# The first product of a second MLP in seven block products for eight, fused with the second product

## The chip, the cores and the metric

The kernel runs on one core of a Trainium2 chip. The metric is device time in microseconds (us), the median of three runs. One further execution was profiled; all rows below come from it.

## The reference

A block retention (a linear attention with decay) feeds two MLPs, all in float32. Cut to what matters here:

```python
x = retention(q, k, v, lam)            # (1536 tokens, 512)
h = x @ moe_w_in                       # (1536, 2048)
x = (np.maximum(h, 0) + alpha * np.minimum(h, 0)) @ moe_w_out
h = x @ moe2_w_in                      # second MLP, first product
r = np.maximum(h, 0.0)
out = (r * r) @ moe2_w_out             # second MLP, second product: (1536, 512)
```

## The kernel before

Each MLP product of float32 operands is made from three matmuls in a faster float32 form: every operand is split into a high part and a low remainder, and low x high, high x low and high x high are added in PSUM.

The retention comes first. Then both MLPs run through one list of steps, 48 for each: a step is one token tile t (512 of 1536 tokens) and one block f of 128 hidden columns. `first` (L176) makes h of a step: 4 chunks of 128 input channels x 3 matmuls = 12 matmuls of 512 columns. `activate` applies the leaky or the squared relu (ScalarE, then VectorE), casts the high part gh on ScalarE (L195), and `rest` subtracts the low part gl on VectorE (L200). `second` (L229, L231) adds the step's share to four running sums in PSUM, 12 matmuls more, two steps later (`LAG`). The order of the steps (`PARTS`) visits a tile in parts; a part's sums that aren't final go through DRAM (`sums`) and are added on VectorE when the next part ends (`end_sum`, L245).

The weights arrive as 64-bit floats and are converted on the chip, one unit (512 values per partition) a step: two activations on ScalarE (L127, L128), three integer operations on VectorE (L134, L135, L143), a cast on ScalarE (L145), a subtraction on VectorE (L154). The sum of the first MLP for a tile stays in PSUM and is split from there into the next x (`next_x`).

The order of instructions on every engine is the order of the code; each engine works its own list in order, and semaphores join them. PSUM has 8 banks: three for h, five for the running sums.

Of the kernel before, what the change touches and what calls it, by code (L numbers as in the profile page):

```python
# [16 lines left out]
CH = 128  # L17
# [6 lines left out]
TT = 512  # L24
# [14 lines left out]
LAG = 2  # L39
ORDER = [(n // B, n % B) for n in range(NN)]  # L40
# [15 lines left out]


@with_exitstack
def retention_then_two_mlps(
# [19 lines left out]
    xp = ctx.enter_context(tc.tile_pool(name="xp", bufs=1))  # L79
    wpa = ctx.enter_context(tc.tile_pool(name="wpa", bufs=1))  # L80
    rawp = ctx.enter_context(tc.tile_pool(name="rawp", bufs=AHEAD))
    bitp = ctx.enter_context(tc.tile_pool(name="bitp", bufs=3))
    gp = ctx.enter_context(tc.tile_pool(name="gp", bufs=LAG + 1))
    tp = ctx.enter_context(tc.tile_pool(name="tp", bufs=1))
    pp = ctx.enter_context(tc.tile_pool(name="pp", bufs=4))
    dram = ctx.enter_context(tc.tile_pool(name="dram", bufs=1, space=bass.MemoryType.DRAM))

    alpha_sb = const.tile([128, NF], F32, name="alpha_sb")

# [110 lines left out]
    def second(m, t, f, part):  # L203
# [4 lines left out]
        if last and f == NF - 2:  # L208
            return
# [424 lines left out]
```

## Time and profile before

| | us |
|---|---|
| timed runs, median (lowest to highest) | 581.49 (581.03 to 581.57) |
| the profiled execution | 582.9 |
| its span, first to last instruction | 580.6 |
| TensorE busy | 572.1 (99%) |
| VectorE busy | 334.7 (58%) |
| ScalarE busy | 293.6 (51%) |

The span is what the profiler saw of instructions; the execution's own time has 2.3 us more around it. A busy share is a mean over stages. Matmuls are pipelined, so the duration listed for one is not the time from one to the next.

### The profile page before, as it was taken

To read this page: it belongs to the slowest core of one execution; us is meant where nothing else is said; L and a number is where in the kernel's file an instruction comes from. 1 tells how busy PE (TensorE), PEld (TensorE's weight loads), DVE (VectorE), ACT (ScalarE), POOL (GpSimd) and SP (SyncE) were. 2 spreads that over 40 slices of the span, in tenths; PEclk is the share of its full clock that TensorE was granted. 3 is DMA by queue.
4 is the path that set the end of the run, shared out by engine and by line. 5 is a ranking of instruction groups with operands and counts; after the bars stand their busy time and mean duration, and the time that the engine had idled before them with its cause. 6 is when DMAs were issued, how large, how long until landed. Compare 5 with 4: busy or idle time off the path is not lost.

```text
span 580.6 us, 7855 instructions
## 1 busy us (share of the span) xinstructions
PE 572.1 (99%) x3058; PEld 475.7 (82%) x3058; DVE 334.7 (58%) x535; ACT 293.6 (51%) x509; POOL 33.3 (6%) x34
## 2 busy tenths in 40 slices
PE   8998999999999999999999999999999999999997
PEld 7887888888888888888888888888888888888885
DVE  3888766666666666866866965665632222222422
ACT  2566765765746765765765654654522222322220
POOL 2785000000000000000000000000000000000000
PEclk9999999999999999999999999999999999999999
DMA  7993343323544223333333123423100000400401
GB/s 255 361 393 120 108 146 109 117 102 109 192 147 168 82 100 109 110 108 110 108 110 109 51 94 110 141 78 109 73 0 1 0 1 0 146 0 1 145 2 72
DMA packets 25732, 62.38 MB, mean 107 GB/s; under 512 B 2904, under 2 KB 3936, under 8 KB 25696
## 3 DMA queue, kind: packets, MB, share of 16 engines
q1 hardware_dynamic: 17488, 32.01, 15.7%
q10 hardware_dynamic: 8208, 29.89, 15.5%
q8 instruction: 24, 0.39, 0.3%
q14 instruction: 12, 0.10, 0.0%
HBM read 52.44 MB, written 9.45 MB: 107 GB/s over the span
## 4 chain that ended last, share of the span: by engine, by line
PE 95%; DMA 3%; DVE 1%; issue 0%; SPq 0%; DVEq 0%
PE h L176 45%; PE acc L231 22%; PE acc L229 22%; PE o L436 2%; PE o L444 2%; PE s L399 1%; DMA q<-in_qt_dram 1%; DMA r<-in_kr_dram 1%; DMA zd<-z 1%; PE pk L459 1%; DMA lam_sb<-in_lam_dram 0%; DVE err L358 0%; DVE ps L245 0%; SPq L304 0%; DVE low L359 0%
## 5 line engine op out<-in xcount | busy, mean ns | idle before, releaser
L195 ACT CAST gh<-g 128x512 fp32r<-128x512 f32 x96 | 59.6, 621 | 90.5 <-DVE g L186 37.5
L186 DVE SCALAR_TENSOR_TENSOR g<-h,g 128x512 f32<-128x512 f32 x48 | 33.2, 691 | 123.4 <-ACT g L185 123.4
L185 ACT ACTIVATE g<-h 128x512 f32<-128x512 f32 x48 | 28.7, 598 | 124.3 <-PE h L176 124.3
L200 DVE TENSOR_TENSOR gl<-g,gh 128x512 fp32r<-128x512 f32 x96 | 66.5, 692 | 30.3 <-ACT gh L195 21.6
L176 PE MATMUL h<-xah,wl 128*128 128x512 f32 x192 | 74.8, 390 | 0.0
L176 PE MATMUL h<-xah,wh 128*128 128x512 f32 x192 | 74.7, 389 | 0.0
L176 PE MATMUL h<-xal,wh 128*128 128x512 f32 x192 | 74.7, 389 | 0.0
L229 PE MATMUL acc<-gh,wl 128*128 128x512 f32 x192 | 74.7, 389 | 0.0
L229 PE MATMUL acc<-gh,wh 128*128 128x512 f32 x192 | 74.7, 389 | 0.0
L229 PE MATMUL acc<-gl,wh 128*128 128x512 f32 x192 | 74.7, 389 | 0.0
L176 PE MATMUL h<-xbh,wl 128*128 128x512 f32 x192 | 74.7, 389 | 0.0
L176 PE MATMUL h<-xbl,wh 128*128 128x512 f32 x192 | 74.7, 389 | 0.0
L176 PE MATMUL h<-xbh,wh 128*128 128x512 f32 x192 | 74.7, 389 | 0.0
L231 PE MATMUL acc<-wl,gh 128*128 128x512 f32 x192 | 74.7, 389 | 0.0
L231 PE MATMUL acc<-wh,gh 128*128 128x512 f32 x192 | 74.7, 389 | 0.0
L231 PE MATMUL acc<-wh,gl 128*128 128x512 f32 x192 | 74.7, 389 | 0.0
L190 DVE SCALAR_TENSOR_TENSOR g<-h,g 128x512 f32<-128x512 f32 x42 | 29.0, 691 | 62.2 <-ACT g L189 62.2
L135 DVE SCALAR_TENSOR_TENSOR bits<-raw,bits 128x512 uint32<-128x512 uint32 x64 | 46.9, 733 | 2.2
L154 DVE TENSOR_TENSOR wl<-bits,wh 128x512 fp32r<-128x512 f32 x64 | 44.6, 697 | 2.7 <-ACT wh L145 2.7
L143 DVE CUSTOM_DVE_ANT_0 bits<-raw,bits 128x1024 uint16<-128x1024 uint16 x64 | 46.0, 718 | 0.0
L127 ACT ACTIVATE bits<-raw 128x512 f32<-128x512 f32 x64 | 43.0, 672 | 0.7 <-DMA raw<-in_w_dram 0.6
L128 ACT ACTIVATE raw<-raw 128x512 int32<-128x512 uint32 x64 | 42.7, 667 | 0.0
(73 smaller groups left out, 786.4 us busy)
## 6 DMA issues: line engine op xcount, KB each, us to landing
raw<-in_w_dram ACTq DMA_DIRECT2D x57, 512.0 KB, 3.3
ps<-sums SPq DMA_DIRECT2D x24, 256.0 KB, 3.1
sums<-p SPq DMA_DIRECT2D x20, 256.0 KB, 2.2
raw<-in_w_dram SPq DMA_DIRECT2D x7, 512.0 KB, 6.3
k<-in_kt_dram SPq DMA_DIRECT2D x12, 256.0 KB, 5.9
q<-in_qt_dram SPq DMA_DIRECT2D x12, 256.0 KB, 5.3
v<-in_vr_dram SPq DMA_DIRECT2D x12, 256.0 KB, 6.0
r<-in_kr_dram SPq DMA_DIRECT2D x10, 256.0 KB, 5.7
```

The costliest lines, as they stand in the source:

```text
L127: nc.scalar.activation(x.bitcast(F32), high.bitcast(F32), AF.Copy, scale=REBIAS)
L128: nc.scalar.activation(low.bitcast(I32), low, AF.Copy, scale=2.0**-29)
L135: nc.vector.scalar_tensor_tensor(x, high, 0x80000000, x, ALU.bitwise_and, ALU.bitwise_or)
L143: nc.vector.tensor_tensor(x.bitcast(I32), x.bitcast(I32), low.bitcast(I32), ALU.add)
L154: nc.vector.tensor_tensor(lo, x, hi.bitcast(F32), ALU.subtract)
L176: nc.tensor.matmul(ph, w[:, cols], x[:, c, :], start=c == 0 and i == 0, stop=c == NC - 1 and i == 2)
L186: nc.vector.scalar_tensor_tensor(g, ph, 0.0, g, ALU.max, ALU.mult)
L190: nc.vector.scalar_tensor_tensor(g, ph, 0.0, g, ALU.max, ALU.subtract)
L195: nc.scalar.copy(gh, g)
L200: nc.vector.tensor_tensor(gl, g, gh.bitcast(F32), ALU.subtract)
L229: nc.tensor.matmul(acc[t][i], w[:, cols], g, **flags)
L231: nc.tensor.matmul(acc[t][i], g[:, cols], w, **flags)
```

## The change

The second MLP's tokens are taken in two tiles of 768 (u = 0, 1) and its hidden columns in eight pairs p of 256. A group n is one u and one p (`GROUPS`: u 0 with p 0 to 3, u 1 with p 0 to 7, u 0 with p 4 to 7). In a group, the 512 input channels, the 256 hidden columns and the 768 tokens are each cut in two, and the 2 x 2 blocks of weights (a) and of x (b) are multiplied in the Winograd form of Strassen's scheme. With s1 = a21 + a22, s2 = s1 - a11, s3 = a11 - a21, s4 = a12 - s2 and t1 = b12 - b11, t2 = b22 - t1, t3 = b22 - b12, t4 = b21 - t2, the seven products are issued in this order:

- P1 = a11 b11 into bank x. ScalarE copies it into bank y (L513).
- P6 = s2 t2 is added in bank y; ScalarE copies the sum out as u2 (L520).
- P2 = a12 b21 is added in bank x, which is then the first quarter of h (relu on ScalarE, L500; squared on VectorE, L501).
- P3 = s3 t3 is added in bank y; ScalarE copies the sum out as u3 (L528).
- P5 = s1 t1 starts bank x again; VectorE adds u3 for another quarter (L535).
- P4 = a22 t4 is added in bank y: another quarter (L500, L501). The two quarters made by L501 are split into halves ga (cast on ScalarE, L505; subtraction on VectorE, L506).
- P7 = s4 b22 is added in bank x; VectorE adds u2 (L544), squares (L547), and the other two quarters are split into gb.

Each product is 2 chunks x 3 matmuls of 384 columns. Between the products stand the six items of the group before (`outputs2`): item j adds block j of 128 tokens to its running sum in bank 2 + j, 6 matmuls of 512 columns (L566). Group 0 has instead the eight items of the first MLP's last two steps, 3 matmuls each (L280).

The weights of the second MLP are converted for two blocks f at a time (`convert_pairs`, lines 318 to 400), with operations of 1024 values, four sums of 256 for s1 to s4, and casts and subtractions of 1024 and 768 values (first product) or 2 x 512 (second). The first MLP's result goes to DRAM (`xs`) and comes back in blocks of 768 values per partition, from which `split_x` makes t1 to t4 and the high and low parts. Both are generators, drawn a few instructions at a time by `fill(us)` at fixed places, each yield being a planned cost; `FILL` holds the five amounts of a group. The first MLP keeps its steps; its conversion now covers its own 32 units alone, and from there on `fill(1.2)` stands ahead of and behind a step. SBUF is four tiles (`low_mem`, `low_r_mem`, `high_mem`, `high_r_mem`) in which `Memory.claim` hands out places by number. The diff, cut to its core:

```diff
 PARTS = [
-    [(0, range(4)), (1, range(4)), (2, range(8)), (1, range(4, 8)), (0, range(4, 16)),
-     (1, range(8, 16)), (2, range(8, 16))],
-    [(0, range(8)), (1, range(8)), (2, range(16)), (1, range(8, 16)), (0, range(8, 16))],
+    (0, range(4)), (1, range(4)), (2, range(8)), (1, range(4, 8)), (0, range(4, 16)),
+    (1, range(8, 16)), (2, range(8, 16)),
 ]
 LAG = 2
+HALF = 384
+NPF = NF // 2
+BLOCKS = 2 * HALF // CH
+GROUPS = [(0, p) for p in range(4)] + [(1, p) for p in range(NPF)] + [(0, p) for p in range(4, NPF)]
+FILL = 1.2, 2.0, 1.2, 0.7, 1.5
...
-STEPS = [(m, t, f, p) for m in range(2) for t, p in PARTS[m] for f in p]
+STEPS = [(t, f, p) for t, p in PARTS for f in p]
 USES = [
-    2 * (NF * STEPS[i][0] + STEPS[i][2]) + half
+    2 * STEPS[i][1] + half
...
+    def convert_pairs():
...
+            nc.vector.tensor_scalar(x, x, 3, None, ALU.logical_shift_left)
+            yield 0.7
+            yield from lows(k - 1)
+            nc.vector.scalar_tensor_tensor(
+                x, both[:, :, 1], 0x80000000, x, ALU.bitwise_and, ALU.bitwise_or
+            )
+            yield 1.2
+            x = x.bitcast(I32)
+            nc.vector.tensor_tensor(x, x, both[:, :, 0].bitcast(I32), ALU.add)
+            yield 1.2
+            raw.pop(k).free()
+            yield from load(k + 2)
+            yield from start(k + 1)
+            if half == 0:
+                a11, a12, a21, a22, s1, s2, s4 = (
+                    bit[k].view(F32)[:, i * DM // 2 : (i + 1) * DM // 2] for i in range(7)
+                )
+                nc.vector.tensor_tensor(s1, a21, a22, ALU.add)
+                nc.vector.tensor_tensor(s2, s1, a11, ALU.subtract)
+                yield 0.8
+                nc.vector.tensor_tensor(a21, a11, a21, ALU.subtract)
+                nc.vector.tensor_tensor(s4, a12, s2, ALU.subtract)
+                yield 0.8
+            done[k] = []
+            for span, at in PAIRS_AT[p % 4][2] if half else PAIRS_AT[p % 4][0:2]:
+                done[k].append((yield from taken(span, at, 2 if half else 7)))
+            for x, hi, lo in cuts(k):
...
+    def split_x(v):
...
+        yield from split("b11", b11)
+        yield minus(b11, b12, b11)
+        yield minus(t2, b22, b11)
+        yield from split("t2", t2)
+        yield from split("b21", b21)
+        yield minus(b21, b21, t2)
+        t2.free()
+        yield minus(b12, b22, b12)
...
+    def fill(us):
+        for gen in list(fillers):
+            while us > 0:
+                cost = next(gen, "end")
+                if cost == "end":
+                    fillers.remove(gen)
+                if cost is None or cost == "end":
+                    break
+                us -= cost
+
...
+    def strassen(n, items):
+
+        u, p = GROUPS[n]
+        v = sum(b <= n for b in begins) - 1
+        banks = (n % 2,), (1 - n % 2,)
+        def product(ps, i, start=False):
+            name, a = WANTED[i]
+            xh, xl = (x.view(F32R, HALF) for x in need(x_parts, (v, name), makers["x", v]))
+            wh, wl = (w.view(F32R) for w in need(pairs, (0, p), makers["w"]))
+            for c in range(2):
+                cols = slice((2 * a + c) * 128, (2 * a + c + 1) * 128)
+                for j, (w, x) in enumerate(((wl, xh), (wh, xl), (wh, xh))):
+                    nc.tensor.matmul(
+                        ps, w[:, cols], x[:, c, :], start=start and c == 0 and j == 0,
+                        stop=c == 1 and j == 2, skip_group_check=True,
+                    )
+            if n in ends:
+                release(x_parts.pop((v, name)))
+
+        def other():
+            item = next(items, None)
+            if item is not None:
+                item()
+
+        def relu_square(out, ps):
+            nc.scalar.activation(out, ps, AF.Relu)
+            nc.vector.scalar_tensor_tensor(out, ps, 0.0, out, ALU.max, ALU.mult)
+
+        def halves(block):
+            hi, lo = borrow(F32R), borrow(F32R)
+            nc.scalar.copy(hi.view(F32R), block.view(F32))
+            nc.vector.tensor_tensor(lo.view(F32R), block.view(F32), hi.view(F32), ALU.subtract)
+            spare[F32].append(block)
+            return hi, lo
+
+        px = bank(f"p1_{n}", banks[0])[:, 0:HALF]
+        product(px, 0, True)
+        py = bank(f"p6_{n}", banks[1])[:, 0:HALF]
+        nc.scalar.copy(py, px)
+        fill(FILL[0])
+        other()
+        other()
+        product(py, 1)
+        us = borrow()
+        u2, u3 = (us.view(F32, HALF)[:, i] for i in range(2))
+        nc.scalar.copy(u2, py)
+        product(px, 2)
+        first_half = borrow()
+        g = first_half.view(F32, HALF)
+        relu_square(g[:, 0], px)
+        fill(FILL[1])
+        other()
+        product(py, 3)
+        nc.scalar.copy(u3, py)
+        fill(FILL[2])
+        other()
+        px = bank(f"p5_{n}", banks[0])[:, 0:HALF]
+        product(px, 4, True)
+        second_half = borrow()
+        h = second_half.view(F32, HALF)
+        nc.vector.tensor_tensor(h[:, 1], px, u3, ALU.add)
+        fill(FILL[3])
+        product(py, 5)
+        relu_square(g[:, 1], py)
+        ga = halves(first_half)
+        other()
+        product(px, 6)
+        if n == visits[p][-1]:
+            release(pairs.pop((0, p)))
+        nc.vector.tensor_tensor(h[:, 0], px, u2, ALU.add)
+        spare[F32].append(us)
+        h = second_half.view(F32)
+        nc.vector.scalar_tensor_tensor(h, h, 0.0, h, ALU.max, ALU.mult)
+        gb = halves(second_half)
+        fill(FILL[4])
+        other()
+        return ga, gb
...
+        def item(j):
+            def run():
+                if n in begins:
+                    acc2[j] = bank(f"acc_{u}_{j}", (2 + j,))
+                gh, gl = (g.view(F32R, HALF) for g in gs[j // 3])
+                w2s = [w.view(F32R) for w in need(pairs, (1, p), makers["w"])]
+                rows = slice(j % 3 * CH, (j % 3 + 1) * CH)
+                for e in range(2):
+                    for i, (w, g) in enumerate(((w2s[2 + e], gh), (w2s[e], gh), (w2s[e], gl))):
+                        nc.tensor.matmul(
+                            acc2[j], g[:, e, rows], w,
+                            start=n in begins and e == 0 and i == 0,
+                            stop=n in ends and e == 1 and i == 2,
+                        )
+                if j % 3 == 2:
+                    spare[F32R].extend(gs[j // 3])
+                if j == BLOCKS - 1 and n == visits[p][-1]:
+                    release(pairs.pop((1, p)))
+                if n in ends:
+                    end_block(n, j)
+
...
+    def end_block(n, j):
+        u, p = GROUPS[n]
+        if n == ends[-1]:
+            block = p2[j]
+            o = block.view(F32)
+            nc.vector.tensor_tensor(o, acc2[j], o, ALU.add)
         else:
-            p = pp.tile([128, 512], F32, tag="p", name=f"p{m}_{t}_{part[0]}_{i}")
...
+    items = last_blocks()
+    for n in range(len(GROUPS)):
...
+        gs = strassen(n, items)
+        for item in items:
+            item()
+        items = outputs2(n, gs)
```

TensorE, second MLP. Before, near the end: the last three matmuls of a step's h (h1_0_15: MLP 1, tile 0, block 15), then the running sums of an earlier step (acc1).

```order
L176 MATMUL h1_0_15_4862<-xbh0_2400,wl62_3809 128x512
L176 MATMUL h1_0_15_4862<-xbl0_2401,wh62_3803 128x512
L176 MATMUL h1_0_15_4862<-xbh0_2400,wh62_3803 128x512
L231 MATMUL acc1_0_8_0_4718<-wl59_3895,gh1_0_13_4814 128x512 [waits Activation_49]
L231 MATMUL acc1_0_8_0_4718<-wh59_3891,gh1_0_13_4814 128x512
L231 MATMUL acc1_0_8_0_4718<-wh59_3891,gl1_0_13_4816 128x512 [waits DVE_49]
L231 MATMUL acc1_0_8_1_4719<-wl59_3895,gh1_0_13_4814 128x512
L231 MATMUL acc1_0_8_1_4719<-wh59_3891,gh1_0_13_4814 128x512
L231 MATMUL acc1_0_8_1_4719<-wh59_3891,gl1_0_13_4816 128x512
```

Now, from P7 of group 0 to item 1 in group 1 (p5_0 is bank x of group 0, p1_1 bank x of group 1; acc2_8 are the first MLP's last sums, acc_0_0 and acc_0_1 the running sums of items 0 and 1 for u = 0).

```order
L487 MATMUL p5_0_2709<-high_r_mem_836 128x384 [waits DVE_49]
L487 MATMUL p5_0_2709<-high_r_mem_836 128x384 x5
L280 MATMUL acc2_8_1_2464<-low_r_mem_67,high_r_mem_836 128x512 x3
L280 MATMUL acc2_8_2_2465<-low_r_mem_67,high_r_mem_836 128x512 x3
L280 MATMUL acc2_8_3_2466<-low_r_mem_67,high_r_mem_836 128x512 x3
L487 MATMUL p1_1_2760<-low_r_mem_67 128x384 [waits DVE_49]
L487 MATMUL p1_1_2760<-low_r_mem_67 128x384 x5
L566 MATMUL acc_0_0_2777<-high_r_mem_836,low_r_mem_67 128x512 [waits Activation_49]
L566 MATMUL acc_0_0_2777<-high_r_mem_836,low_r_mem_67 128x512
L566 MATMUL acc_0_0_2777<-high_r_mem_836,low_r_mem_67 128x512 [waits DVE_49]
L566 MATMUL acc_0_0_2777<-high_r_mem_836,low_r_mem_67 128x512 x3
L566 MATMUL acc_0_1_2784<-high_r_mem_836,low_r_mem_67 128x512 [waits DVE_49]
```

Before, only gh and gl are waited for; now P7, P1 and the bank of item 1 wait for VectorE as well.

VectorE, second MLP. Before, the last steps: squaring, subtraction, and the last additions (ps1).

```order
L186 SCALAR_TENSOR_TENSOR g1_0_13_4811<-h1_0_13_4798,g1_0_13_4811 128x512 [waits Activation_49]
L200 TENSOR_TENSOR gl1_0_13_4816<-g1_0_13_4811,gh1_0_13_4814 128x512 [waits PE_49,Activation_49]
L186 SCALAR_TENSOR_TENSOR g1_0_14_4843<-h1_0_14_4830,g1_0_14_4843 128x512 [waits Activation_49]
L200 TENSOR_TENSOR gl1_0_14_4848<-g1_0_14_4843,gh1_0_14_4846 128x512 [waits PE_49,Activation_49]
L186 SCALAR_TENSOR_TENSOR g1_0_15_4875<-h1_0_15_4862,g1_0_15_4875 128x512 [waits Activation_49]
L200 TENSOR_TENSOR gl1_0_15_4880<-g1_0_15_4875,gh1_0_15_4878 128x512 [waits PE_49,Activation_49]
L245 TENSOR_TENSOR ps1_0_0_4882<-acc1_0_8_0_4718,ps1_0_0_4882 128x512 [waits DMAHW6_49,DMAHW2_49,PE_49]
L245 TENSOR_TENSOR ps1_0_1_4883<-acc1_0_8_1_4719,ps1_0_1_4883 128x512 [waits DMAHW7_49,DMAHW3_49,PE_49]
L245 TENSOR_TENSOR ps1_0_2_4884<-acc1_0_8_2_4720,ps1_0_2_4884 128x512 [waits DMAHW4_49,DMAHW0_49,PE_49]
L245 TENSOR_TENSOR ps1_0_3_4885<-acc1_0_8_3_4721,ps1_0_3_4885 128x512 [waits DMAHW5_49,DMAHW1_49,PE_49]
```

Now, group 0 from the filler ahead of its second squaring to its end (low_mem rows are weight conversion, acc2_8 rows the first MLP's last additions).

```order
L359 TENSOR_TENSOR low_r_mem_67<-low_mem_66,low_r_mem_67 128x512 [waits Activation_49]
L501 SCALAR_TENSOR_TENSOR high_mem_835<-p6_0_2662,high_mem_835 128x384 [waits Activation_49]
L506 TENSOR_TENSOR low_r_mem_67<-high_mem_835,low_r_mem_67 128x768 [waits Activation_49]
L301 TENSOR_TENSOR high_mem_835<-acc2_8_0_2463,high_mem_835 128x512 [waits DMAHW0_49,PE_49]
L544 TENSOR_TENSOR high_mem_835<-p5_0_2709,high_mem_835 128x384 [waits PE_49]
L547 SCALAR_TENSOR_TENSOR high_mem_835<-high_mem_835 128x768 [waits DVE_49]
L506 TENSOR_TENSOR low_r_mem_67<-high_mem_835,low_r_mem_67 128x768 [waits Activation_49]
L374 SCALAR_TENSOR_TENSOR low_mem_66<-low_mem_66 128x1024
L379 ISA low_mem_66<-low_mem_66 128x2048 [waits DVE_49]
L301 TENSOR_TENSOR high_mem_835<-acc2_8_1_2464,high_mem_835 128x512 [waits DMAHW1_49,PE_49]
L301 TENSOR_TENSOR high_mem_835<-acc2_8_2_2465,high_mem_835 128x512 [waits DMAHW2_49,PE_49]
L301 TENSOR_TENSOR high_mem_835<-acc2_8_3_2466,high_mem_835 128x512 [waits DMAHW3_49,PE_49]
```

Before, the last additions stand alone at the end of the kernel; now those of the first MLP stand among the operations of group 0, behind filler.

## Rows read from the trace of the kernel before

**Rows 1.** The page: busy time by engine; the chain that ended last, by engine.
```profile
PE 572.1 (99%) x3058; PEld 475.7 (82%) x3058; DVE 334.7 (58%) x535; ACT 293.6 (51%) x509; POOL 33.3 (6%) x34
...
PE 95%; DMA 3%; DVE 1%; issue 0%; SPq 0%; DVEq 0%
```

**Rows 2.** Waits of TensorE, whole span: for whom, us in total, times, longest.
```profile
PE o L436 <- issue: 1.6, 1, 1.6
```

**Rows 3.** The chain in order of time: start us, us, what.
```profile
65.51 2.72 PE h L176 x12
...
568.71 8.17 PE acc L231 x36
```

**Rows 4.** Timeline, the last instruction of VectorE.
```profile
576.91 0.69 DVE L245 TENSOR_TENSOR ps<-acc,ps 128x512 f32<-128x512 f32 x1 [0.67 <-PE acc L231]
```

**Rows 5.** Timeline of TensorE, retention: start, us, line, op, weights, columns, count.
```profile
13.08 2.05 PE L318 MATMUL warm_ps<-warm 128*128 128x128 f32 x16
...
25.47 0.69 PE L459 MATMUL pk<-v,r 128*64 128x64 f32 x16
26.08 1.16 PE L399 MATMUL s<-q,k 64*128 64x128 f32 x16
27.18 1.09 PE L436 MATMUL o<-sc,v 128*64 128x128 f32 x16
28.20 0.98 PE L444 MATMUL o<-q,state 64*64 64x128 f32 x14
```

**Rows 6.** Span and mean granted clock of TensorE, 1 being the full 2.4 GHz.
```profile
core 0: 580.6 us, clock 1.000
```

**Rows 7.** Groups of VectorE by form: shapes, count, busy us, mean ns, idle before.
```profile
L200 DVE TENSOR_TENSOR gl<-g,gh 128x512 fp32r<-128x512 f32 x96 | 66.5, 692 | 30.3 <-ACT gh L195 21.6 <-PE acc L231 2.7 <-PE acc L229 0.7
L135 DVE SCALAR_TENSOR_TENSOR bits<-raw,bits 128x512 uint32<-128x512 uint32 x64 | 46.9, 733 | 2.2
L143 DVE CUSTOM_DVE_ANT_0 bits<-raw,bits 128x1024 uint16<-128x1024 uint16 x64 | 46.0, 718 | 0.0
...
L134 DVE TENSOR_SCALAR bits<-bits 128x512 uint32<-128x512 uint32 x64 | 28.3, 442 | 0.1
...
L411 DVE TENSOR_TENSOR sc<-s,dec 128x1024 f32<-128x1024 f32 x10 | 12.1, 1214 | 0.4 <-PE s L399 0.4
...
L485 DVE TENSOR_TENSOR state<-pk,old 128x256 f32<-128x256 f32 x8 | 3.3, 413 | 1.1 <-PE pk L459 1.1
```

**Rows 8.** Groups of ScalarE by form.
```profile
L195 ACT CAST gh<-g 128x512 fp32r<-128x512 f32 x96 | 59.6, 621 | 90.5 <-DVE g L186 37.5 <-DVE g L190 32.4 <-DVE g L193 18.3
L127 ACT ACTIVATE bits<-raw 128x512 f32<-128x512 f32 x64 | 43.0, 672 | 0.7 <-DMA raw<-in_w_dram 0.6
...
L189 ACT ACTIVATE g<-g,alpha_sb 128x512 f32<-128x512 f32 x42 | 30.4, 725 | 1.4
...
L404 ACT COPY sc<-s 128x1024 f32<-128x1024 f32 x2 | 2.0, 1012 | 5.5 <-PE s L399 5.5
```

**Rows 9.** Timeline of VectorE and of ScalarE, instructions that wait for nothing.
```profile
328.36 0.69 DVE L200 TENSOR_TENSOR gl<-g,gh 128x512 fp32r<-128x512 f32 x1
328.97 0.69 DVE L154 TENSOR_TENSOR wl<-bits,wh 128x512 fp32r<-128x512 f32 x1
...
331.95 0.62 ACT L145 CAST wh<-bits 128x512 fp32r<-128x512 f32 x1
...
332.48 0.67 ACT L127 ACTIVATE bits<-raw 128x512 f32<-128x512 f32 x1
```

**Rows 10.** Timeline, last matmul of a step's h and the relu behind it.
```profile
562.88 0.39 PE L176 MATMUL h<-xbh,wh 128*128 128x512 f32 x1
...
563.31 0.60 ACT L185 ACTIVATE g<-h 128x512 f32<-128x512 f32 x1 [3.46 <-PE h L176]
```

**Rows 11.** DMA issues of the raw weights: count, KB each, median us to landing.
```profile
raw<-in_w_dram ACTq DMA_DIRECT2D x57, 512.0 KB, 3.3
```

**Rows 12.** Groups of the weight loads, which overlap the matmuls.
```profile
L176 PEld LDWEIGHTS h<-xbh,wh 128*128 128x128 f32 x192 | 36.1, 188 | 7.4
```

More of the change, by code (lines that the diff above doesn't have):

```diff
@@ new lines, in retention_then_two_mlps, with release, borrow, first @@
+    last_of_f = {f: s for s, (t, f, part) in enumerate(STEPS)}
+    last_of_t = {t: s for s, (t, f, part) in enumerate(STEPS)}
+    g_of, acc, p_of = {}, {}, {}
+    sums = dram.tile([NTILE, 4, 128, TT], F32, name="sums")
+    xs = dram.tile([NC, 128, B * S], F32, name="xs")
+    def release(blocks):
+        for block in blocks:
+            block.free()
+    spare = {F32R: [mem.claim(LOW_R, GR + 3 * i, 3) for i in range(8)]}
+    def borrow(kind=F32):
+        return spare[kind].pop(0)
+    def first(s):
+        t, f, part = STEPS[s]
+        wh, wl = (w.view(F32R) for w in weights[2 * f])
+        xh, xl = (x.view(F32R, TT) for x in xt[t])
+        ph = bank(f"h{t}_{f}", (0, 1, 2))
@@ new lines, in retention_then_two_mlps, with need @@
+    fillers = []
+    def fill(us):
[7 more added lines that the diff above has]
+                us -= cost
+    def need(table, key, gen):
+        while key not in table:
+            cost = next(gen)
+            assert cost is not None, (key, "no room")
+        return table[key]
+    makers = {}
@@ new lines, in retention_then_two_mlps @@
+    mem.add(high.tile([128, SIZES[HIGH] * KB], F32, name="high_mem"))
+    mem.add(high.tile([128, SIZES[HIGH_R] * KB], F32R, name="high_r_mem"))
+    spare[F32] = [mem.claim(HIGH, G + 3 * i, 3) for i in range(3)]
+    spare["p"] = [mem.claim(HIGH, G + 9 + 2 * i, 2) for i in range(4)]
+    makers["w"] = convert_pairs()
+    for s in range(len(STEPS)):
+        t, f, part = STEPS[s]
+        sums_end = s >= LAG and STEPS[s - LAG][1] == STEPS[s - LAG][2][-1]
+        unit = conv.k < 2 * NF and not sums_end
+        if unit:
+            conv.start(conv.k + 1)
+            conv.begin()
+        elif conv.k == 2 * NF:
+            if makers["w"] not in fillers:
+                fillers.append(makers["w"])
+            fill(1.2)
+        ph = first(s)
+        g, gh = activate(s, ph, unit or conv.k == 2 * NF)
+        if unit:
+            conv.middle()
+            if conv.k + 3 == 2 * NF:
+                next(makers["w"])
+        rest(s, g, gh)
+        if unit:
+            conv.end()
+        elif conv.k == 2 * NF:
+            fill(1.2)
+        if f == part[-1] and part[0] > 0:
+            load_sums(t)
+        if s >= LAG:
+            second(s - LAG)
+        if s == last_of_t[1] + LAG:
+            makers["x", 0] = split_x(0)
+            fillers.insert(0, makers["x", 0])
@@ L577 @@
+    for item in items:
+        item()
 _INS = ["qt", "kt", "vr", "kr", "lam", "w1", "alpha", "w2"]
```

370 lines of the change are left out of this document (235 added, 135 removed).

## The prediction

> **What bounds the kernel now.** Read the page's totals and its chain first: TensorE is busy for 572.1 of 580.6 us and holds 95% of the chain that ended last [rows 1]. The list of who waited for whom, cut to TensorE, has nothing after 54.4 us: its four waits stand at lines of the retention stage and its warm-up, the longest single one 1.6 us [rows 2]. So from the first matmul of the first MLP to the last of the second, the time is a count of matmuls times their spacing. The chain in order of time gives the spacing: 12 matmuls of 512 columns in 2.72 us, 226.7 ns each, and the last 36 of them in 8.17 [rows 3]. 2304 make 522.3 us, the stretch from 54.4 to 576.7. The "389 ns" of such a matmul in the table of groups is its latency, not its price. After the last matmul comes one addition on VectorE that starts at 576.91, and a store; the span ends at 580.6, so the tail behind the last matmul is 3.9 us [rows 4, 6].
>
> VectorE and ScalarE are off this path, but they are FIFO neighbours of it: what they finish late, TensorE waits for. That is where this change can lose what it wins.
>
> **What the change removes: matmuls.** The first product of the second MLP was 48 steps of 12 matmuls, 576 x 226.7 ns = 130.6 us. Now there are 16 groups (768 tokens by 256 hidden columns), each with seven products of 6 matmuls of 384 columns: 672 matmuls. No row shows 384 columns. Three neighbours bound it: start to start, 16 matmuls of 64 columns take 0.61 us (38 ns each), 16 of 128 take 1.10 or 1.02 us (69 or 64 ns), and 512 columns take 226.7 [rows 3, 5]. At 2.4 GHz (granted clock 1.000 [rows 6]) the columns alone are 26.7, 53.3 and 213.3 ns, so 11 to 15 ns come on top whatever the size. For 384 I take 160 + 13.3 = 173.3 ns. The ends: three quarters of 226.7 is 170; a straight line from 69 at 128 columns to 226.7 gives 174. The weights don't forbid it: the warm-up matmuls, which load 128x128 weights each time, take 2.05 us for 16, so they follow at 128 ns at the most [rows 5]. 672 x 173.3 = 116.5 us, so the matmuls **save 14.1 us** (13.7 to 16.3). The second product stays 576 matmuls of 512 columns; the first MLP and the retention stage keep theirs.
>
> The Trainium skill ("TensorE: Matmul & The Clock Gate", section "Back-to-back issue gap") puts the spacing at columns by 2.4 GHz plus 2.5 ns. By it 512 columns would take 215.8 ns, where the trace has 226.7; with its figure at both sizes the estimate of the saving is 15.1 us. The rows decide for 13.3 ns on top.
>
> **What it adds, and where it is hidden.** Durations come from rows and grow with the elements. VectorE: 256 elements 0.413 us, 512 0.692, 1024 1.214; so 384 is 0.56 and 768 0.95 [rows 7]. ScalarE: 512 0.62, 1024 1.012; so 384 is 0.49 to 0.52, 768 0.83 [rows 8]. An instruction that waits for nothing starts 0.08 to 0.09 before the listed end of the one ahead: two subtractions of 512 lie 0.61 apart (listed 0.69), a cast and its follower 0.53 (listed 0.62) [rows 9]. A result of TensorE reaches ScalarE 0.43 us after its last matmul's start, 0.20 after the next could start [rows 10].
>
> Per group of 15.44 us (42 x 173.3 ns + 36 x 226.7 ns) the fixed work is 5 us on VectorE and 4 on ScalarE. The rest is filler: the weight conversion in pairs and three splits of x. A pair costs VectorE twice a shift, a merge and an addition of 1024 values (0.7, 1.25 and 1.2 us, scaled from L134, L135 and L143), four sums of 256 and subtractions of 1024, 768, 512 and 512: 11.5 us; ScalarE four activations of 1024 (1.1, from L127) and casts: 7.5 us. Five pairs are left for the groups. A split of x is 11 subtractions of 768 on VectorE; two of the three lie in groups. Neither engine is full over a group; only the position of filler in the two FIFOs matters. The trip of x through DRAM (12 stores, 12 loads) lies beside the last eight steps of the first MLP, 43 us, and costs nothing; each raw load (two of 512 KB, 3.3 us to land when alone [rows 11]) is issued one piece ahead, at least 4.7 us before use. In the first MLP the filler sits before and after a step's own VectorE work; a step's gl is due three stretches of 2.72 us after its h, and the chain of five operations to it takes 3.3 us [rows 7, 8, 10], which leaves 4.8 us, so I cost it at nothing; if that cover goes, each late microsecond shows at the second product's wait for gl.
>
> In an undisturbed group, with P1 starting at 0, P6 may start at 3.76 and needs ScalarE's copy of P1's sum; P7 may start at 13.04 and needs VectorE's addition on P5. The copy could end at 1.7, so some 1.5 to 2 us of filler may stand in front of it.
>
> Group 0 is the tight one. Its second-product items are 3 matmuls, not 6, so it lasts 12.72 us, while VectorE has 22 instructions, 16.7 us of listed work, in it: filler, the group's own work and four last additions of the first MLP. I follow VectorE from P1's start. The first MLP's last h was ready 2.52 us before it, so its gl is done at 0.9. Filler (2.7 us) up to 3.6; the squaring on P2 at 5.7; then a merge, an addition, a shift, held until ScalarE's activation at 7.9, and a subtraction, held until its cast at 9.4: 10.1. The addition on P5 ends at 10.64; P7, which needs it, was due at 9.64: **1.1 us** with the hand-over. Then come ga, the first late addition (14.1), h0, the squaring (15.6), ScalarE's cast (16.5), gb's subtraction (17.4), two filler instructions (19.7) and only then the addition that empties acc2_8_1 (20.4). That tile has bank 3, which the running sum acc_0_1, the second item of group 1, takes over. TensorE is there at 16.2: **4.3 us**.
>
> Groups 1 to 2: after the cast of gb (35.2 on the same clock) ScalarE has two halves of a conversion of 1024 elements (2.0) and two casts (1.05) in front of the copy, which ends at 38.75; P6 was due at 37.2: **1.55 us**. The same place in front of P6 of groups 4 and 12 (two casts of 768), 5 (two casts and a block copy) and 8 (two halves of a conversion) gives 0.65, 0.65, 0.55 and 1.3: **3.15 us**. The other groups have no filler there, or less than their slack; one P4, in group 9, waits 0.1.
>
> A copy from PSUM to PSUM on ScalarE has no row; 0.42 to 0.62 us are its ends (384 elements start to start, or a full 512), which moves these five places by 0.1 each. I take 0.42, the nearer size.
>
> Sum: -14.1 + 1.1 + 4.3 + 1.55 + 3.15 + 0.1 = **-3.9 us**. Tail and head stay. Against the profiled execution's own 582.9 us (580.6 span and 2.3 around it) that is 579.0; the median of the timed runs is 581.49, 1.4 below the profiled one, so the forecast is **577.6 us**.
>
> **Rivals.**
> 1. The waits are smaller. If the large operations overlap more than the rows' 0.08 us, or the late addition of group 0 comes some microseconds earlier, only half of the 10.2 us of waits is left: 572.5; with none, 567.4. For it: VectorE is busy for only 58% of the span now [rows 1], and all places but two exceed their slack by under 1.6 us. Against: the chain through group 0 is one dependent sequence, with no gap to win.
> 2. Slower: filler in front of the copy and of the bank's release eats more than the matmuls save. If every operation holds its engine for its whole listed duration, the same walk gives 0.2 + 1.4 + 4.9 in groups 0 and 1, 2.7 at group 2, 1.5, 1.1, 2.3 and 1.5 at groups 4, 5, 8 and 12, and 2.2 at P4 of groups 7 and 9 and P6 of 7: 17.8 us, and 581.5 - 14.1 + 17.8 = 585.2. It decides from 14.1 us of waits on. Against it stand the overlaps in [rows 9]; a load of raw weights that lands late adds to it.
> 3. The clock. The longest pause of TensorE in the trace after its start is 1.6 us [rows 2], and the granted clock was 1.000 throughout [rows 6]; the 4.3 us here has no row. If it brings 1.2 GHz for as long as the pause itself, half of that, 2.15 us, is lost: 579.8. The Trainium skill (same page, section "Why this matters for your kernels") advises against idle gaps between bursts of matmuls, since they bring the lower clock back; by that rule this rival holds, and no run here shows it yet.
> 4. The weights set the spacing after all: a weight load is listed at 188 ns [rows 12], longer than 173.3. Then 672 x 188 = 126.3, the saving is 4.2, every group is 0.6 us longer, the waits shrink to some 8.5, and the time is 585.8. Against it: the 128 ns of the warm-up, whose loads are as large.
>
> **How the numbers follow.** Forecast 0.45, rival 1 0.20, rival 2 0.20, rival 3 0.10, rival 4 0.05. No change means within 0.2%, 1.2 us, about what a measurement of this kernel can tell. The forecast's own band, 573.5 to 581.5, comes from the spacing's ends (-2.2 to +0.4) and 3.5 us either way on the waits: 0.41 faster, 0.03 same, 0.01 slower. Rival 1 is faster. Rival 2 is slower but for 0.04 within the bound, rival 3 splits 0.06 and 0.04, rival 4 is slower. Together: faster 0.67, same 0.11, slower 0.22. The range 570.5 to 585.5 leaves out the better part of rival 1 below and the far ends of rivals 2 and 4 above.
>
> **What the profile after would show.** The spacing of the 384-column matmuls within one product (173 ns; 188 would be rival 4). From the start of group 0 to the end of the last matmul: 252.5 us of matmuls (12.72 + 15 x 15.44 + 8.16) plus the waits. TensorE's waits: one of about 4 us on VectorE at the second-product line at the start of group 1, one of 1 us on VectorE at P7 of group 0, and some five of 0.5 to 1.6 us on ScalarE's copy of P1. TensorE's granted clock after the long one. The forecast is wrong if the waits together are far from 10 us, if TensorE waits in the first MLP, or if the waits name DMA.

## The result and the profile after

The changed kernel takes **584.23 us** (median of five runs, 583.80 to 585.26) where the kernel before takes 581.49 (580.61 to 581.73): a ratio of 1.0054, with a 95% interval of 1.0039 to 1.0068. The forecast was 577.6 us, a gain. The measured time lies inside the stated range (570.5 to 585.5), but on the other side of no change. The profiled execution took 584.18 us.

Page of the changed kernel: busy time by engine, the granted clock in 40 slices, the chain by engine, and the groups of the 512-column matmuls of the second product (L566) and of the first MLP (L280).

```profile
PE 565.3 (97%) x3154; PEld 485.4 (83%) x3154; DVE 380.3 (65%) x552; ACT 308.9 (53%) x506; POOL 34.1 (6%) x34
...
PEclk9999999999999999999999899999999999999999
...
PE 82%; DVE 7%; ACT 5%; DMA 3%; issue 2%; SPq 0%; DVEq 0%
...
L566 PE MATMUL acc<-low_r_mem 128*128 128x512 f32 x288 | 73.0, 393 | 0.0
...
L280 PE MATMUL acc<-low_r_mem 128*128 128x512 f32 x288 | 69.3, 389 | 0.0
```

Beside [rows 1] the chain went from 95% TensorE to 82%, with VectorE and ScalarE now on it. One slice has a lower clock. And one row should make the reader stop: the same kind of matmul, 512 columns, is listed at 393 ns in the second product and at 389 in the first MLP. The waits of TensorE, against [rows 2]:

```profile
PE p L487 <- ACT p L513: 5.2, 5, 1.4
PE acc L566 <- DVE high_mem L301: 4.0, 1, 4.0
...
PE p L487 <- DVE high_mem L535: 0.9, 1, 0.9
```

They are the seven that the prediction named. The timeline of TensorE from group 0 to P6 of group 2 (start us, us, ..., count, idle before) has three of them:

```profile
308.92 1.23 PE L487 MATMUL p<-low_r_mem,high_r_mem 128*128 128x384 f32 x6
...
319.78 1.31 PE L487 MATMUL p<-high_r_mem 128*128 128x384 f32 x6 [0.86 <-DVE high_mem L535]
323.01 1.23 PE L487 MATMUL p<-low_r_mem 128*128 128x384 f32 x6
324.08 1.55 PE L566 MATMUL acc<-high_r_mem,low_r_mem 128*128 128x512 f32 x6
329.61 2.93 PE L566 MATMUL acc<-high_r_mem,low_r_mem 128*128 128x512 f32 x6 [3.98 <-DVE high_mem L301]
332.34 2.43 PE L487 MATMUL p<-low_r_mem 128*128 128x384 f32 x12
...
344.33 1.21 PE L487 MATMUL p<-low_r_mem 128*128 128x384 f32 x6
345.38 2.92 PE L566 MATMUL acc<-low_r_mem 128*128 128x512 f32 x12
349.61 2.38 PE L487 MATMUL p<-low_r_mem 128*128 128x384 f32 x12 [1.31 <-ACT p L513]
```

Start to start is the price: item 1 was due 1.39 us after item 0, at 325.47, and came at 329.61, 4.14 late. Then its own six matmuls took 2.73 us, where six others take 1.39, and the next twelve 2.26 (332.34 to 334.60) for 2.09. The windows of that stretch say why (stretch, its length, PE, PEld, DVE, ACT and POOL busy, granted clock, DMA share, GB/s):

```profile
326.00:328.00 2.00, 0.00 (x0) 0.00 (x0) 1.97 (x3) 2.00 (x2) 0.00 (x0) 1.00 0.00 0
328.00:330.00 2.00, 0.39 (x1) 0.39 (x2) 2.00 (x3) 0.08 (x1) 0.00 (x0) 0.81 0.00 0
330.00:332.00 2.00, 2.00 (x6) 1.52 (x6) 1.97 (x6) 0.00 (x0) 0.00 (x0) 0.50 0.82 301
332.00:334.00 2.00, 2.00 (x11) 1.90 (x10) 0.21 (x1) 0.19 (x1) 0.00 (x0) 0.83 1.03 322
```

TensorE stood still, the granted clock fell to 0.50 (1.2 GHz), and the matmuls behind the pause ran at half speed for some 3 us: 1.5 us lost beside the wait itself.

The undisturbed group shows the third loss. Timeline of TensorE: a stretch of the first MLP, a whole group from P1 to the next P1, and the end.

```profile
102.11 2.88 PE L234 MATMUL h<-low_r_mem 128*128 128x512 f32 x12
104.83 2.88 PE L280 MATMUL acc<-low_r_mem 128*128 128x512 f32 x12
...
426.34 1.20 PE L487 MATMUL p<-low_r_mem,high_r_mem 128*128 128x384 f32 x6
427.38 2.92 PE L566 MATMUL acc<-low_r_mem 128*128 128x512 f32 x12
430.14 2.27 PE L487 MATMUL p<-low_r_mem,high_r_mem 128*128 128x384 f32 x12
432.25 1.55 PE L566 MATMUL acc<-low_r_mem 128*128 128x512 f32 x6
433.64 1.21 PE L487 MATMUL p<-low_r_mem,high_r_mem 128*128 128x384 f32 x6
...
441.98 1.20 PE L487 MATMUL p<-low_r_mem,high_r_mem 128*128 128x384 f32 x6
...
568.60 1.55 PE L566 MATMUL acc<-low_r_mem 128*128 128x512 f32 x6
569.99 8.33 PE L566 MATMUL acc<-high_r_mem,low_r_mem 128*128 128x512 f32 x36
```

The 384-column matmuls are close to what was expected (12 in 2.11 or 2.09 us, 6 in 1.04: 173 to 176 ns). Those of 512 columns are not: 12 take 2.76 us and 6 take 1.39 between products (230 to 232 ns), but 12 take 2.72 in the first MLP, as in [rows 3]. The last 36 show it within one line: listed at 8.33 us from the first start to the last end, they follow at (8.33 - 0.39) / 35 = 227 ns. So the group takes 15.64 us, not 15.44; 0.16 of the 0.20 lie on the 512 columns, 0.04 on the 384. The tail is as in [rows 4]: the last addition starts at 578.36, 3.7 us before the end of the span.

### The profile page after: what moved, and what is told of

Its sections match the earlier page's. It is cut to its first block, busy times and chain, and to the rows that moved or that the text cites. A ratio compares the mean times of both kernels' runs of the same rounds, so it can differ in the third digit from the quotient of the medians.

```text
span 582.1 us, 8021 instructions
## 1 busy us (share of the span) xinstructions
PE 565.3 (97%) x3154; PEld 485.4 (83%) x3154; DVE 380.3 (65%) x552; ACT 308.9 (53%) x506; POOL 34.1 (6%) x34
## 4 chain that ended last, share of the span: by engine, by line
PE 82%; DVE 7%; ACT 5%; DMA 3%; issue 2%; SPq 0%; DVEq 0%
PE h L234 22%; PE acc L280 22%; PE acc L566 17%; PE p L487 16%; PE o L763 2%; PE o L771 2%; ACT low_r_mem L505 1%; PE s L726 1%; DMA q<-in_qt_dram 1%; ACT low_r_mem L427 1%; DVE high_mem L547 1%; DVE low_r_mem L506 1%; ACT low_mem L343 1%; PE pk L786 1%; DMA r<-in_kr_dram 1%
## 5 line engine op out<-in xcount | busy, mean ns | idle before, releaser
L566 PE MATMUL acc<-high_r_mem,low_r_mem 128*128 128x512 f32 x288 | 73.8, 398 | 4.0 <-DVE high_mem L301 4.0
L566 PE MATMUL acc<-low_r_mem 128*128 128x512 f32 x288 | 73.0, 393 | 0.0
L280 PE MATMUL acc<-low_r_mem,high_r_mem 128*128 128x512 f32 x288 | 69.8, 390 | 0.0
L280 PE MATMUL acc<-low_r_mem 128*128 128x512 f32 x288 | 69.3, 389 | 0.0
L234 PE MATMUL h<-low_r_mem,high_r_mem 128*128 128x512 f32 x288 | 69.2, 389 | 0.0
L234 PE MATMUL h<-low_r_mem 128*128 128x512 f32 x288 | 69.0, 390 | 0.0
L566 PEld LDWEIGHTS acc<-high_r_mem,low_r_mem 128*128 128x128 f32 x288 | 54.2, 190 | 13.8 <-DVE high_mem L301 4.4
L280 PEld LDWEIGHTS acc<-low_r_mem 128*128 128x128 f32 x288 | 54.0, 188 | 11.4 <-DVE high_mem L301 0.2
L234 PEld LDWEIGHTS h<-low_r_mem,high_r_mem 128*128 128x128 f32 x288 | 54.1, 188 | 11.2
L280 PEld LDWEIGHTS acc<-low_r_mem,high_r_mem 128*128 128x128 f32 x288 | 54.0, 188 | 10.9
L566 PEld LDWEIGHTS acc<-low_r_mem 128*128 128x128 f32 x288 | 53.4, 188 | 9.0
L487 PE MATMUL p<-low_r_mem,high_r_mem 128*128 128x384 f32 x288 | 55.7, 337 | 3.6 <-ACT p L513 3.6
L487 PE MATMUL p<-low_r_mem 128*128 128x384 f32 x288 | 55.9, 337 | 1.6 <-ACT p L513 1.6
L505 ACT CAST low_r_mem<-high_mem 128x768 fp32r<-128x768 f32 x32 | 26.7, 835 | 51.8 <-DVE high_mem L547 39.4
L506 DVE TENSOR_TENSOR low_r_mem<-high_mem,low_r_mem 128x768 fp32r<-128x768 f32 x32 | 30.7, 958 | 28.9 <-ACT low_r_mem L505 28.9
L501 DVE SCALAR_TENSOR_TENSOR high_mem<-p,high_mem 128x384 f32<-128x384 f32 x32 | 17.8, 556 | 39.2 <-ACT high_mem L500 39.2
```

Of the source, the lines that this page charges most:

```text
L234: nc.tensor.matmul(ph, w[:, cols], x[:, c, :], start=c == 0 and i == 0, stop=c == NC - 1 and i == 2)
L280: nc.tensor.matmul(acc[t][i], w[:, cols], g, start=f == part[0] and j == 0, stop=f == part[-1] and j == 2,)
L487: nc.tensor.matmul(ps, w[:, cols], x[:, c, :], start=start and c == 0 and j == 0, stop=c == 1 and j == 2, skip_group_check=True,)
L501: nc.vector.scalar_tensor_tensor(out, ps, 0.0, out, ALU.max, ALU.mult)
L505: nc.scalar.copy(hi.view(F32R), block.view(F32))
L506: nc.vector.tensor_tensor(lo.view(F32R), block.view(F32), hi.view(F32), ALU.subtract)
```

## The experiments

Each run was timed beside the kernel before, and its ratio is to that. The changed kernel was not timed beside them, so a gain against it is also read from the traces, as the time from the first matmul of group 0 to the start of the last one (269.0 us in the changed kernel).

**The pause at item 1.** e1 deals the banks so that item 1 gets one that has been empty since the first MLP.

```diff
-acc2[j] = bank(f"acc_{u}_{j}", (2 + j,))
+acc2[j] = bank(f"acc_{u}_{j}", ((2, 6, 7, 3, 4, 5)[j],))
```

> Only the banks of the six accumulators of the second product are dealt differently: item 1 gets bank 6, which stands empty since the first MLP, and the late bank 3 goes to item 3. Theory A (the changed kernel's start is late because item 1 of group 1 needs a bank that VectorE empties late, 4.0 us, and the clock falls to 0.56 behind the pause and costs another 1.5 us): the wait of 4.0 at L566 on VectorE's L301 goes, the clock's windows from 327 to 333 us read 1.00, and the time is 584.2 - 4.0 - 1.5 = 578.7 us (578 to 580). Rival B (the pause only stands for VectorE's backlog after the first MLP, whoever meets it): the wait shows again at the next instruction of group 1 that needs VectorE, P4's or P5's bank, with 2 to 4 us, and the time stays at 582 to 584. Rival C (the low clock has a cause of its own): the wait goes and the clock is still below 1.00 for some us there; 580.2.

Measured: 582.19 us, ratio 0.9997 (0.9986 to 1.0008): about 2 us gained of 5.5 (2.1 in the traces). Timeline of e1 around P6 of group 2, and the window behind its pause:

```profile
340.68 2.92 PE L566 MATMUL acc<-low_r_mem 128*128 128x512 f32 x12
346.35 3.70 PE L487 MATMUL p<-low_r_mem 128*128 128x384 f32 x12 [2.75 <-ACT p L513]
```
```profile
346.00:348.00 2.00, 1.65 (x5) 1.65 (x6) 1.87 (x3) 0.30 (x1) 0.00 (x0) 0.50 0.46 168
```

The wait at L566 is gone and group 1 ran at full clock, but it still took 16.48 us, 0.84 more than an undisturbed group. P6 of group 2, 1.47 us late before, was now 2.91 late, and the clock fell behind this pause instead. Theory A and rival B each held for a part. The time stayed where B had it, but its wait came a group later than B put it, at ScalarE's copy. VectorE and ScalarE stay late with that wait removed, and the next wait shows.

**The filler at the end of the group.** e2 moves it behind the copy that P6 waits for (1.5 less planned at the end of a group, 1.2 more at the start of the next).

```diff
-FILL = 1.2, 2.0, 1.2, 0.7, 1.5
+FILL = 2.4, 2.0, 1.2, 0.7, 0
```

> The filler work that stood at the end of each group on ScalarE (the amount 1.5, ahead of the copy of P1's bank at L513) is moved to the first place in the next group, behind that copy (2.4 for 1.2). Theory A (the copy is late because this filler, with its chain over VectorE, stands ahead of it): the five waits of P6 on L513, 5.2 us together, go, nothing else changes, 584.2 - 5.2 = 579.0 us (578 to 580). Rival B (ScalarE and VectorE have no room for the filler in the shorter group wherever it stands): the waits move to the copies and sums behind it, u2 at P7 or P4, or to the group where the block is needed, and the time stays within 583 to 585.

Measured: 576.36 us, ratio 0.9898 (0.9879 to 0.9918), better than theory A asked; in the traces it is 7.7 us less than the changed kernel. The longest wait of TensorE in e2:

```profile
PE acc L566 <- DVE high_mem L301: 2.1, 1, 2.1
```

All five waits on L513 are gone: groups 2, 4, 5, 8 and 12 take 15.64 us, and only groups 3 and 11 take 0.3 more. The pause at item 1 halved as well: in the changed kernel two instructions of filler (L374, L379) stand on VectorE between gb's subtraction and L301, and in e2 L301 follows that subtraction at once. With that one edit the change is faster than the kernel before.

**The clock.** e4 keeps the wait and fills it with matmuls whose result nobody uses.

```diff
         fill(FILL[0])
         other()
+        if n == 1:
+            ...
+            for i in range(18):
+                nc.tensor.matmul(pw, wh[:, 0:128], xh[:, 0:512], start=True, stop=True)
         other()
```

> In group 1, between item 0 and the item that waits 4.0 us for VectorE, TensorE gets 18 more matmuls of 512 columns into an idle bank, whose result nobody uses: 18 x 226.7 ns = 4.08 us, just the pause. The wait stays where it was in time, but TensorE works through it. Theory A (the pause itself lowers the clock, and this costs 1.5 us): the granted clock stays at 1.00 from 327 to 333 us, the six matmuls of item 1 take 1.36 to 1.39 instead of 2.73 us, and the time is 584.2 - 1.5 = 582.7 us. Rival B (the slow stretch of 2.8 us after the pause has another cause, such as the bank being shared with VectorE's late sums): the stretch is slow again and the time is 584.2 or up to 0.2 above.

Measured: 582.89 us, ratio 1.0016 (1.0007 to 1.0026) for 1.0054 of the changed kernel. Timeline of TensorE and one window of e4:

```profile
324.01 1.23 PE L487 MATMUL p<-low_r_mem 128*128 128x384 f32 x6
...
326.46 4.25 PE L521 MATMUL idle<-low_r_mem 128*128 128x512 f32 x18
330.61 1.67 PE L572 MATMUL acc<-high_r_mem,low_r_mem 128*128 128x512 f32 x6
332.12 2.25 PE L487 MATMUL p<-low_r_mem 128*128 128x384 f32 x12
```
```profile
330.00:332.00 2.00, 2.00 (x10) 1.40 (x9) 2.00 (x4) 0.00 (x0) 0.00 (x0) 1.00 0.32 110
```

Item 1 starts 6.60 us after P1, to the hundredth as without the extra matmuls (329.61 - 323.01), and group 1 is 1.4 us shorter (19.93 for 21.32 from P1 to P1). So here the pause lowers the clock, and nothing else in that stretch does. The Trainium skill ("TensorE: Matmul & The Clock Gate", section "Why this matters for your kernels") warns of idle gaps between bursts of matmuls for this reason; the trace agrees, at 1.4 to 1.5 us for this pause. Not every execution pays it for a shorter one: of e1's ten, three had a mean granted clock of 0.999 or 1.000 and took 580.46 to 580.74 us, the seven others 0.994 to 0.998 and 581.92 to 582.53. That the three kept the clock behind the pause is argued from these means; those executions were not profiled.

**The 0.2 us of each group.** e5 draws the items in pairs behind P1, P2 and P4: three runs of 512 columns in a group for five.

```diff
         fill(FILL[1])
         other()
+        other()
         product(py, 3)
         ...
         fill(FILL[2])
-        other()
         ...
         ga = halves(first_half)
         other()
+        other()
         product(px, 6)
         ...
         fill(FILL[4])
-        other()
```

> The six items of the second product (six matmuls of 512 columns each) are drawn in three pairs per group, after P1, P2 and P6... P5's sum, instead of 2+1+1+1+1: three runs of 512 columns between the block products of 384 columns for five, with the same matmuls. Theory A (the 0.2 us by which an undisturbed group is above 42 x 173.3 + 36 x 226.7 = 15.44 is paid at each change between 384 and 512 columns, 0.04 for each run): the undisturbed group goes from 15.64 to 15.56 us, so 16 x 0.08 = 1.3 us less. Rival B (it is paid per matmul, each one of 512 columns 5 ns slower than before): 15.64 stays, and a run of 12 takes 2.78. Beside it the waits of P6 on L513 and those of P5 on VectorE can change by some tenths each, since the pairs move the times at which the copies are wanted; the period of the undisturbed groups (6, 10, 13 to 15) decides, not the total.

Measured: 585.22 us, ratio 1.0052 (1.0032 to 1.0072). Timeline of TensorE in e5, one undisturbed group:

```profile
426.39 1.20 PE L487 MATMUL p<-low_r_mem,high_r_mem 128*128 128x384 f32 x6
427.44 2.92 PE L566 MATMUL acc<-low_r_mem 128*128 128x512 f32 x12
...
432.30 2.92 PE L566 MATMUL acc<-low_r_mem 128*128 128x512 f32 x12
435.06 3.31 PE L487 MATMUL p<-low_r_mem,high_r_mem 128*128 128x384 f32 x18
438.21 2.92 PE L566 MATMUL acc<-low_r_mem 128*128 128x512 f32 x12
...
442.04 1.20 PE L487 MATMUL p<-low_r_mem,high_r_mem 128*128 128x384 f32 x6
```

15.65 us: fewer changes of size won nothing in the group, and theory A in its simple form fell. (The total did not fall either; other waits grew, those on L513 from 5.2 to 7.3 us.) But a price for each 512-column matmul does not fit, since the last 36 of the changed kernel follow at 227 ns. The starts of single matmuls show where the 0.2 us are. A run of 12 of 512 columns is 0.04 above 2.72 where a run of 6 is 0.03 above 1.36, and the last three of the 12 follow at 227 ns again. The products behind a run of 12 are 0.03 above their sum, be it 12 of them (2.11 for 2.08) or 18 (3.15 for 3.12); those behind a run of 6 are less than 0.01 above it. So the price lies on the first matmuls behind a change and depends on the length of both runs: e5 pays 0.12 for 0.16 on the 512 columns, but 0.08 for 0.04 on the 384.

e7 has the edits of e1 and e2 and takes the change of size away: the matmuls of the second product write 384 columns, all but the first of each sum. It leaves the last 128 columns of the output out of the sum.

```diff
+wide = n in begins and e == 0 and i == 0
+cut = 512 if wide else 384
 nc.tensor.matmul(
-    acc2[j], g[:, e, rows], w,
+    acc2[j][:, 0:cut], g[:, e, rows], w[:, 0:cut],
```

> As the kernel with both edits, but the matmuls of the second product write 384 of their 512 columns (except the first of each accumulator): the last 128 columns of the second MLP's output are left out of the sum. Nearly every matmul from 320 us on then has the same moving size. Theory A (the 0.2 us by which a group is above its sum is paid after each change between 384 and 512 columns): an undisturbed group takes 78 x 173.3 ns = 13.52 us, and runs of 12 take 2.08. Rival B (it comes from what the other engines do beside it, from the banks or from the operands): 13.7 us, with matmuls of 175 to 176 ns. Groups in which VectorE or ScalarE, now short of time, keep TensorE waiting are left aside.

Measured: 552.96 us, one run, of which only the length of a group is used. Timeline of TensorE in e7, around an undisturbed group:

```profile
399.01 1.20 PE L487 MATMUL p<-low_r_mem 128*128 128x384 f32 x6
400.05 2.24 PE L568 MATMUL acc<-low_r_mem 128*128 128x384 f32 x12
402.13 2.24 PE L487 MATMUL p<-low_r_mem 128*128 128x384 f32 x12
...
412.53 1.20 PE L487 MATMUL p<-low_r_mem,high_r_mem 128*128 128x384 f32 x6
```

412.53 - 399.01 = 13.52 us, the sum to the hundredth. With one size of matmul, the same banks and tiles and the same work on the other engines, the extra is gone. It belongs to the mix of 384 and 512 columns; by what mechanism was not settled.

**Both edits, and what is left.** e3 joins e1 and e2.

> Both edits together: the empty bank 6 for item 1, and the filler of the group's end moved behind the copy of the next group. Each alone left a pause of 2 to 3 us in groups 1 and 2 with a low clock behind it (e1: 2.75 us at P6 of group 2; e2: 2.1 us at item 1 of group 1). Theory A (the two pauses have these two causes, and the clock only follows a pause): both go, the clock reads 1.00 from 305 us to the end, every group from 1 on takes 15.64 us, and the time is e2's 576.4 less 2.1 for the wait, 1.5 for the clock and 0.5 beside it: 572.3 us (571.5 to 573.5). Rival B (VectorE is behind after the first MLP by about 2 us whatever the order, and somebody must wait for it): a wait of 1 to 2.5 us at P5 or P7 of group 1 or at P6 of group 2, with the clock again below 1.00: 575 to 576.5.

Measured: 575.27 us, ratio 0.9882 (0.9867 to 0.9897): rival B in time and in the size of the wait. Timeline of TensorE in e3:

```profile
310.14 1.23 PE L487 MATMUL p<-low_r_mem,high_r_mem 128*128 128x384 f32 x6
...
333.44 1.33 PE L487 MATMUL p<-low_r_mem 128*128 128x384 f32 x6 [1.75 <-ACT high_mem L520]
```

The wait moved once more, to P3 of group 1, where neither theory had it, and the clock stayed at 1.00 behind it, against rival B. e6 is e3 with the pairs of e5.

> The two edits of the kernel before this one, and the items drawn in three pairs. The pairs alone did not change the undisturbed group (15.64 us with three runs of 512 columns as with five). Theory A (what a change of the moving size costs grows with the length of the run it begins, and is spread over its first matmuls, so longer and fewer runs give the same): 15.64 again, and the time is that of the kernel before this one within 0.5 us, 572 to 573. Rival B (the waits in the run of pairs hid a gain of 0.08 for each group): 15.56, and 1.2 us less than the kernel before this one.

Measured: 574.84 us, ratio 0.9871 (0.9852 to 0.9890). An undisturbed group takes 15.64 us again (419.46 to 435.10), so theory A on the period; its total missed, as e3's did.

e8 is e3 with `fill(FILL[0] * (n != 1))`, e9 is e3 with `fill(FILL[0] * (n > 1))`, and e10 is e6 with the edit of e8.

> As the kernel with both edits, but in group 1 the first place for filler (2.4 behind the copy of P1's bank) is left empty; its work comes in the next places. In the kernel with both edits P3 of group 1 waits 1.75 us for the copy u2 at L520, which stands on ScalarE behind a filler cast (L398) that waited 1.45 us for VectorE. Theory A (this filler is the last cause of a pause in the start): the wait goes and P1 of group 2 comes 1.9 us earlier: 575.3 - 1.9 = 573.4 us (572.7 to 574.2). Rival B (VectorE's work after the first MLP is late by this much whatever stands where): the wait moves once more, to P5 or P6 of group 1 or 2, with 1 to 2 us, and the time stays at 574.5 to 575.5.

> As the kernel before this one, and the first place is left empty in group 0 too. In group 0 P5 waits 0.54 us for u3's copy L528 behind filler on ScalarE and P7 about 0.2 us for VectorE. Theory A: these 0.7 us go as well, 572.7 us (572 to 573.5). Rival B (the filler left out here is wanted for group 1 and comes back as a wait of 1 us or more in group 1): 573.5 to 575.

> The same empty first place in group 1, with the items drawn in three pairs. The pairs had waits of 0.5 and 0.3 us in groups 1 and 2 and 0.6 in group 0. Theory A (the wait of 0.5 at the copy of P1's bank in group 1 is filler): 574.8 - 0.5 to 1.0 = 574.1 us, the undisturbed group 15.64. Rival B (the two orders differ by what a change between 384 and 512 columns costs): 15.56 for the group and up to 1.2 us below e8.

Measured: e8 574.00 us, ratio 0.9855 (0.9839 to 0.9870); e9 579.12, ratio 0.9945 (0.9929 to 0.9960); e10 **573.28**, ratio 0.9845 (0.9829 to 0.9861). The one wait of TensorE in e9 behind the retention stage:

```profile
PE acc L566 <- DVE high_r_mem L359: 5.4, 1, 5.4
```

In e8 group 1 takes 15.75 us, as theory A had it, and waits of 0.8 and 0.5 us are left in groups 4 and 0. e9 cleared groups 0 and 1, and both theories missed what followed: in group 4 the first item waited 5.4 us for a subtraction that makes its weights (L359), and the clock fell with that too (0.58 from 372 to 376 us, 0.57 from 376 to 380). That the filler left out in two groups was not caught up by then is argued from the order of the work, not tried. e10 beats both kernels, by 1.55% the kernel before; its undisturbed group is 15.64 again (402.32 to 417.96).

## Why the prediction was wrong

**Right.** The matmuls' saving: products at 174 ns, and rival 4's 188 as a spacing is refuted, though a weight load is still listed at 188 to 190. All seven places where TensorE came half a microsecond or more late stood where they were put, and where VectorE and ScalarE were followed instruction by instruction the sizes held: P7 of group 0 1.05 late (1.1 forecast), item 1 4.14 (4.3), P6 of group 2 1.47 (1.55), groups 5 and 8, by their length, 0.53 and 1.06 (0.55 and 1.3). The first MLP waits for nothing, and no wait in the groups names a DMA. So none of the prediction's own signs of being wrong came up; they did not look at the 512-column matmuls.

**Luck.** "11 to 15 ns come on top whatever the size" (10 to 15, by the same rows) is not what [rows 5] shows. Its matmuls of 64 and 128 columns have weights 64 wide or 64 deep; the one row there with the products' 128*128 weights, the warm-up, has up to 128 ns for 128 columns, 75 above the columns alone. That the 13.3 ns of the 512 columns held for 384 is what this run measured, not what those rows could promise. And rival 2's 585.2 us is nearer to the measured time than the forecast, but its mechanism did not come: it wants 17.8 us of waits, and there are 11.85. Rival 1's smaller waits did not come either. (The lower end of the forecast's own band, 573.5, is not the sum of its parts, which is 571.9; nothing here hangs on it.)

**The steps that failed**, from the start of group 0 to the end of the last matmul: 262.7 us forecast (252.5 and 10.2 of waits), 269.2 measured.

1. "Per group of 15.44 us (42 x 173.3 ns + 36 x 226.7 ns)". The spacings were taken from stretches of one size and added. Mixed, the group takes 15.64: 15 x 0.20 = 3.0 us, and 0.3 more in group 0. No row of before could price it, since its matmuls from the first MLP on all have 512 columns; it should have been named as unknown and bounded. e7, with one size, takes the sum to the hundredth. The Trainium skill ("TensorE: Matmul & The Clock Gate", section "Back-to-back issue gap") also gives the gap as a function of the number of columns alone, for an isolated matmul; 226.7 alone and 230 in the mix show that here it depends on the neighbours.
2. The 0.65 us each for groups 4 and 12: by their length 1.62 and 1.65 measured, 2.0 more together. The walk took the two casts ahead of the copy and overlooked the cast ahead of the relu. Timeline of the changed kernel ahead of P6 of group 4 (the operations up to 376 us are group 3's):

```profile
372.38 1.83 DVE L420 TENSOR_TENSOR high_mem<-high_mem 128x768 f32<-128x768 f32 x2
...
374.24 0.83 ACT L427 CAST low_r_mem<-high_mem 128x768 fp32r<-128x768 f32 x1 [2.64 <-DVE high_mem L420]
...
374.98 0.49 ACT L500 ACTIVATE high_mem<-p 128x384 f32<-128x384 f32 x1
...
380.62 1.56 ACT L427 CAST low_r_mem<-high_mem 128x768 fp32r<-128x768 f32 x2
...
382.09 0.47 ACT L513 COPY p<-p 128x384 f32<-128x384 f32 x1
```

   The cast waited 2.64 us for a subtraction of the split, the relu of P4 queued behind it, and the whole chain of ga and gb to the copy came about 1 us later. This is read from the timeline; no run tried it apart.
3. The sum has no term for the clock. Rival 3, given 0.10, happened: 1.55 us where it said 2.15, and e4 shows that the pause is its cause. Once a pause of 4.3 us was forecast, the clock belonged into the sum.

The sum with the measured terms: -14.1 + 11.85 (seven waits of 11.5 and small ones) + 3.3 + 1.55 = +2.6 us; the medians differ by 2.74. So the sign was lost by the 5 us of steps 1 and 3, with step 2 on top. Of the miss of 6.6, 6.5 lie between group 0 and the last matmul. Group 0 itself began at 308.92, 1.2 us earlier than the prediction's count gives (54.4 + 1128 x 0.2267), while the forecast took 1.4 off because the profiled execution of before was that much above its median, and the changed kernel's is at its median; these two nearly cancel. The start is not a mark of the kernel: in e3, with the same code ahead of it, group 0 began at 310.14.

## What to carry to other kernels

A time built from matmul spacings needs a row in which the sizes stand mixed as they will be; spacings of separate stretches need not add up. When TensorE's work is cut, look at the in-order engines behind it first: moving one amount of filler was worth nearly 8 us here, more than the change lost, and a kernel with fewer matmuls was slower until it was moved. And a wait that is taken away tells where the next one stands: follow the late engine, not the instruction that waits for it.

## What the runs showed of the hardware that was not expected

- Behind a change between 384 and 512 columns the first matmuls follow slower: six of 512 in 1.39 us for 1.36, twelve in 2.76 for 2.72, the last three of them at 227 ns again. How much is paid depends on the run ahead too: 0.03 us for the 384 columns behind twelve of 512, under 0.01 behind six. With one size the sum holds to 0.01 us in 13.52.
- A pause of TensorE cost more than itself: 4.1 us of waiting at item 1 brought 1.4 to 1.5 us of half-speed matmuls behind it.
- A copy of 384 values from PSUM to PSUM on ScalarE is listed at 0.47 us, and the next instruction starts 0.41 behind it (382.09 to 382.50). No row of before had it; 0.42 was assumed.
